# A fused top-k attention and Fourier-mix kernel: fewer key and value loads, and the attention output transposed by the DMA queue

## The chip, the cores and the metric

The kernel runs on one core of one Trainium2 chip. The metric is device time in microseconds for one execution of the whole program; less is better. The core has a matrix engine (TensorE, PE in the profile, with its weight loads shown apart as PEld), a vector engine (VectorE, DVE), an activation engine (ScalarE, ACT), a general engine (GpSimd, POOL) and SyncE (SP), which here does nothing but issue DMAs. Each engine works through its own list of instructions in order; where an instruction needs a result of another engine it waits, and everything behind it on the same engine waits too.

## The reference

Two blocks one after the other. Sizes: 8 batches, 8 heads, 576 tokens, head size 64; the model width is 512, and the hidden width of the MLP 2048. All is float32.

```python
def _attn_ref(q, k, v):
    scores = scale * np.matmul(q, k.transpose(0, 1, 3, 2))
    kth = np.partition(scores, -top_k, axis=-1)[..., -top_k:-top_k + 1]   # top_k = 32
    scores = np.where(scores >= kth, scores, -1000000000.0)
    scores = scores - np.max(scores, axis=-1, keepdims=True)
    attn = np.exp(scores)
    attn = attn / (np.sum(attn, axis=-1, keepdims=True) + 1e-09)
    return np.matmul(attn, v)

def _moe_ref(x, w_ch1, w_ch2):          # x: heads side by side, (8, 576, 512)
    X = np.fft.fft(np.fft.fft(x, axis=1), axis=2)
    u = x + np.real(X)
    un = (u - mean(u)) / np.sqrt(var(u) + 1e-06)
    return u + np.maximum(un @ w_ch1, 0.0) @ w_ch2
```

## The kernel before

The attention is worked in 32 pairs of heads (4 pairs to a batch). A pair has 9 items (`IN_PAIR`): the 576 queries are cut into four blocks of 128, of which each head is an item, and one block of 64 tail queries, in which both heads share an item. So there are 288 items, and the main loop (L1468) makes one step `i` for each: in step i VectorE finds the 32 largest scores of item i and begins those of item i+1 (four MAX8 and three MATCH_REPLACE8 per item, L406 and L408), while TensorE makes the scores of item i+3 (L382, L352), and ScalarE and GpSimd mask item i-1 (`mask`, L427 on ScalarE, L430 on GpSimd). `bounds` (L415) is one small GpSimd operation per item that turns the 32 maxima into the threshold `nt`; the mask of the next step needs it.

From pair 4 on, but for pairs 7 and 31 (`by_dma`), the probabilities are turned by DMA: ScalarE splits an item's float32 numbers into two planes of 16-bit words (`plane`, L451), SyncE writes them to DRAM (L464, or L466 to L468 for the tail item), and one step later issues a DMA transpose back into SBUF (`turn`, L484, tile `PT`). With them `attend` (L542) multiplies by the values. It runs for two chunks of a pair: chunk 0 (320 queries: two blocks and the tail) and chunk 1 (256 queries). Its result `o` lies in PSUM with the head dimension on the partitions, so it has to be turned once more and divided by the row sums. Before the change that is done so: in the step of `attend`, ScalarE copies `o` to `xT` (L556) and `rd` holds the reciprocals (L569); in a later step `to_tokens` has TensorE transpose `xT` into a PSUM tile `tpx` (L582, three transposes for chunk 0, two for chunk 1), and VectorE multiplies `tpx` by `rd` into `x` (L586, and L593 for the tail rows). For batch 1 the multiplication is on ScalarE (L605).

When a batch's attention is done, its `x` goes through the Fourier mix (GpSimd adds, `fold_ops`; TensorE products, L733, L790, L794), the normalisation, and the two layers of the MLP (L944; L971, L1010, L1141). The MLP is a list of units; each step takes so many units from the list as a planner (`level`, `fixed_cost`) finds room for beside the attention of later batches. The units of batch b are put on the list at its "arrival", a fixed number of steps after the step `T0` (L1360), so TensorE works on the MLP of one batch while the attention of the next ones runs. After the last item only the MLP of the last batch and what is left of the one before it remain.

SyncE's list in a step is: `turn` of item i-3, the planes of item i-2, pieces of the second weight matrix that units bring in (`bring`, L887), the loads of keys, queries or values for later pairs (`load_nat`, `load_v`: L237, L267, L277), and stores of results. GpSimd's list in a step is: the mask of item i-1, whatever is planned under "pool0" (folds), some sums for the MLP, `bounds(i)`, and more sums.

A chunk waits in the list `pending` until `to_tokens` may run: the step after its `attend`, no step with another `attend` in it, and for batches 2 and later only when the batch two before it has been stored, since `x` has two buffers.

Of the kernel before, what the change touches and what calls it, by code (L numbers as in the profile page):

```python
# [73 lines left out]
def kernel(  # L74
# [157 lines left out]

    def load_half(dst, src, pair, e, h, queue=None):

        b, hp = divmod(pair, NPB)
        s2 = src[b, 2 * hp + e].rearrange("(h r) d -> h r d", h=2)
        (queue or nc.sync).dma_start(  # L237
            out=dst[:, 2 * h:2 * h + 2, e, :],
            in_=s2[h, 0:2 * P, :].rearrange("(t p) d -> p t d", p=P),
        )  # L240

    def load_full(dst, src, pair):
        for e in range(2):
            for h in range(2):
                load_half(dst, src, pair, e, h)

    def load_tails(dst, src, pair, row0=(0, 0), queue=None, heads=(0, 1)):
        b, hp = divmod(pair, NPB)
        for e in heads:
            s2 = src[b, 2 * hp + e].rearrange("(h r) d -> h r d", h=2)  # L250
            for h in range(2):
                r0 = row0[e] + TH * h
                (queue or nc.sync).dma_start(
                    out=dst[r0:r0 + TH, NF, e, :], in_=s2[h, 2 * P:HS, :]
                )

    def heads_of(src, pair):
        b, hp = divmod(pair, NPB)
        return src[b, 2 * hp:2 * hp + 2].rearrange("e (h r) d -> h e r d", h=2)

    def load_nat(n, pair):
        if pair < NPAIR:
            nat[n, pair] = nat_t
            src = q if n == "q" else k
            load_full(nat_t, src, pair)
            for h in range(2):
                nc.sync.dma_start(  # L267
                    out=nat_t[TH * h:TH * (h + 1), NF, :, :],
                    in_=heads_of(src, pair)[h, :, 2 * P:HS, :].rearrange("e r d -> r e d"),
                )  # L270

    def load_v(pair):
        if pair < NPAIR:
            v_of[pair] = v_t[pair % 2]
            load_full(v_of[pair], v, pair)
            for e in range(2):
                nc.sync.dma_start(  # L277
                    out=v_of[pair][TAIL * e:TAIL * (e + 1), NF, e, :],
                    in_=heads_of(v, pair)[:, e, 2 * P:HS, :],
                )  # L280

# [40 lines left out]
    def scores(i, part):  # L322
# [14 lines left out]
        plain = (slice(0, NF * P), slice(NF * P, S))  # L337
        if e is None:
            to = [(Ssb[i], slice(TAIL * h, TAIL * (h + 1)), *plain) for h in range(2)]
        else:  # L340
            to = [
                (Ssb[i], slice(0, P), *plain),
                (Ssb[i + 1], slice(0, P), slice(TAIL, S), slice(0, TAIL)),
# [14 lines left out]
        if e is None and i >= PER_BATCH:  # L358
# [13 lines left out]
            for h, (s_t, r, _, _) in enumerate(to):  # L372
                for g in range(2):
                    nc.scalar.copy(  # L374
                        out=s_t[r, half * g:half * (g + 1)],
# [42 lines left out]

    def by_dma(i):

        pair = i // PER_PAIR
        return NPB <= pair < NPAIR - 1 and pair != 2 * NPB - 1
# [22 lines left out]
    def plane(i, half):  # L445
# [19 lines left out]
        else:  # L465
            nc.sync.dma_start(out=to[:, :, 0:S], in_=words[0:nq])  # L466
            nc.sync.dma_start(out=to[:, :, S:S + TAIL], in_=words[nq:P, :, NF * P:S])
            nc.sync.dma_start(out=to[:, :, S + TAIL:2 * S], in_=words[nq:P, :, 0:NF * P])  # L468
# [82 lines left out]
    def attended(pair, ch, late):  # L551
# [3 lines left out]
        xT = attp.tile([P, CW[0]], F32, name=f"xT_{pair}_{ch}", tag="xT", bufs=4)  # L555
        nc.scalar.copy(out=xT[:, 0:w], in_=o[:, 0:w])  # L556
        xT_of[pair, ch] = xT
# [14 lines left out]
    def to_tokens(pair, ch, at_once=True):  # L572
# [5 lines left out]
        xT, rd = xT_of.pop((pair, ch)), rd_of.pop((pair, ch))  # L578
        shape, name = [P, 4, P], f"tpx_{pair}_{ch}"
# [3 lines left out]
        cols = slice(P * hp, P * (hp + 1))  # L583
# [772 lines left out]
    for b in range(B):  # L1356
# [3 lines left out]
        T0 = end + (2 if first else 3 if soon else 4 if last else 5)  # L1360
# [107 lines left out]
    while i < N + 5 or plan or queue or sums:  # L1468
# [25 lines left out]

        if pending and pending[0][0] <= i and (
            i < 2 * PER_BATCH + 4 or chunk_at(i)[0] is None
        ):
            _, pp, pc = pending[0]
            if pp // NPB < 2 or pp // NPB - 2 in written:
                pending.pop(0)  # L1500
                tok.append(lambda: to_tokens(pp, pc, not short))
# [84 lines left out]
        for where in ("pool", "pool2", "load", "load2"):  # L1586
# [41 lines left out]
```

## Time and profile before

| | us |
|---|---|
| median of 3 runs | 1900.37 |
| lowest and highest of them | 1894.85, 1901.92 |
| the profiled execution | 1894.46 |
| its span, first to last instruction | 1892.7 |

The profile is of one execution. Its busy times per engine are sums over the span; an engine that is busy 90% of the time need not be the one that all wait for in every stage, so the stages are also shown one by one. In a list of waits, a line reads: engine and line that waited, the arrow, what it waited for, then us in total, number of waits, longest. In a table of windows each engine has its busy time and, in brackets, its instructions; PEclk is the clock that TensorE was granted, as a share of full speed. In a timeline a row is: start, us, engine, line, operation, out<-in, count, and in square brackets the idle time before it.

### The profile page before, as it was taken

To read this page: it belongs to the slowest core of one execution; us is meant where nothing else is said; L and a number is where in the kernel's file an instruction comes from. 1 tells how busy PE (TensorE), PEld (TensorE's weight loads), DVE (VectorE), ACT (ScalarE), POOL (GpSimd) and SP (SyncE) were. 2 spreads that over 40 slices of the span, in tenths; PEclk is the share of its full clock that TensorE was granted. 3 is DMA by queue.
4 is the path that set the end of the run, shared out by engine and by line. 5 is a ranking of instruction groups with operands and counts; after the bars stand their busy time and mean duration, and the time that the engine had idled before them with its cause. 6 is when DMAs were issued, how large, how long until landed. Compare 5 with 4: busy or idle time off the path is not lost.

```text
span 1892.7 us, 27288 instructions
## 1 busy us (share of the span) xinstructions
PE 1720.7 (91%) x8134; PEld 1086.8 (57%) x8134; DVE 1580.9 (84%) x3301; ACT 1296.3 (68%) x3104; POOL 911.6 (48%) x1278
## 2 busy tenths in 40 slices
PE   5667699889899999999999999999999999999999
PEld 3344364365456654566456665666556655667677
DVE  7999999699899999997998998998999999862110
ACT  6878658577787777776777687767787778652100
POOL 4768643354745356354643565355544465341012
PEclk8878899899899999999999999999999999999999
DMA  5333026561567755585465854585456755430132
GB/s 166 106 93 108 20 63 167 155 158 32 137 154 191 179 132 131 135 208 141 123 157 135 228 123 124 146 218 145 124 147 172 198 129 144 122 116 6 50 101 80
DMA packets 521972, 249.19 MB, mean 132 GB/s; under 512 B 403680, under 2 KB 511841, under 8 KB 521825
## 3 DMA queue, kind: packets, MB, share of 16 engines
q1 hardware_dynamic: 521040, 247.24, 50.1%
q8 instruction: 65, 1.06, 0.2%
q14 instruction: 83, 0.67, 0.1%
q10 hardware_dynamic: 784, 0.21, 0.0%
HBM read 93.63 MB, written 84.74 MB: 94 GB/s over the span
## 4 chain that ended last, share of the span: by engine, by line
PE 64%; DVE 11%; ACT 9%; DMA 6%; POOL 5%; issue 3%; SPq 2%; POOLq 0%; DVEq 0%; ACTq 0%
PE hp L944 23%; PE cp L971 9%; PE o L542 8%; DVE m L406 5%; PE sp L382 5%; DVE wk L408 5%; PE yp L733 3%; PE cw L1141 3%; PE cv L1141 3%; PE cp L1010 3%; ACT wk L451 2%; POOL wk L430 2%; ACT wk L427 2%; DMA PT<-planes 2%; PE sp_t L352 2%
## 5 line engine op out<-in xcount | busy, mean ns | idle before, releaser
L430 POOL TENSOR_TENSOR wk<-S,wk 128x576 f32<-128x576 f32 x288 | 408.1, 1417 | 570.0 <-ACT wk L427 564.7
L406 DVE MAX8 m<-wk 128x8 f32<-128x576 f32 x864 | 626.7, 750 | 6.0
L944 PE MATMUL hp<-unT,w 128*128 128x256 f32 (+1 forms) x2048 | 533.9, 411 | 3.3 <-ACT hT L948 2.5
L944 PEld LDWEIGHTS hp<-unT,w 128*128 128x128 f32 x2048 | 378.0, 191 | 133.7 <-issue 29.9
L408 DVE MATCH_REPLACE8 wk<-m,wk 128x576 f32<-128x576 f32 x576 | 427.5, 742 | 0.0
L451 ACT COPY wk<-S 128x576 uint16<-128x576 uint16 x468 | 288.7, 666 | 0.1
L427 ACT ACTIVATE wk<-S,nt 128x576 f32<-128x576 f32 x288 | 222.3, 772 | 72.1 <-POOL nt L415 71.1
L971 PE MATMUL cp<-w,hT 128*128 128x512 f32 x512 | 247.8, 621 | 0.0
L406 DVE MAX8 m<-S 128x8 f32<-128x576 f32 x288 | 214.0, 743 | 34.5 <-ACT S L356 34.3
L542 PE MATMUL o<-PT,v 128*64 128x256 f32 (+3 forms) x1440 | 206.4, 430 | 24.9 <-DMA PT<-planes 16.7
L408 DVE MATCH_REPLACE8 wk<-m,S 128x576 f32<-128x576 f32 x288 | 213.6, 742 | 0.0
L438 ACT ACTIVATE S<-wk,nt 128x576 f32<-128x576 f32 x234 | 182.6, 781 | 43.8 <-POOL wk L430 42.6
L948 ACT ACTIVATE hT<-hp 128x320 f32<-128x320 f32 (+1 forms) x256 | 103.6, 410 | 151.5 <-PE hp L944 150.8
L382 PE MATMUL sp<-kT,qT 64*128 64x512 f32 (+1 forms) x528 | 180.3, 680 | 13.1 <-ACT means L1329 5.1
L542 PEld LDWEIGHTS o<-PT,v 128*64 128x64 f32 x1440 | 118.5, 158 | 110.5 <-issue 30.1
L971 PEld LDWEIGHTS cp<-w,hT 128*128 128x128 f32 x512 | 94.1, 197 | 110.4 <-issue 108.6
L385 ACT COPY S<-sp 128x512 f32<-128x512 f32 (+1 forms) x264 | 141.8, 587 | 18.1 <-PE sp L382 17.2
L1086 POOL TENSOR_TENSOR hT<-hT 128x512 f32<-128x512 f32 x64 | 81.4, 1275 | 99.3 <-ACT hT L948 86.4
L415 POOL TENSOR_TENSOR nt<-m,cc 128x2 f32<-128x2 f32 x288 | 58.6, 204 | 117.9 <-DVE m L406 113.9
L352 PE MATMUL sp_t<-kt,qT 128*128 128x128 f32 x320 | 71.9, 308 | 44.8 <-ACT S L374 27.4
L352 PEld LDWEIGHTS sp_t<-kt,qT 128*128 128x128 f32 x320 | 55.6, 197 | 99.2 <-ACT S L374 41.7
L1141 PE MATMUL cw<-w,hT 128*128 128x256 f32 x448 | 105.8, 383 | 0.9 <-issue 0.6
(160 smaller groups left out, 2130.4 us busy)
## 6 DMA issues: line engine op xcount, KB each, us to landing
planes<-wk SPq DMA_DIRECT2D x208, 288.0 KB
w<-w_parts SPq DMA_DIRECT2D x82, 512.0 KB
space<-in_moe_w_ch_dram SPq DMA_DIRECT2D x32, 512.0 KB
nat<-in_q_dram SPq DMA_DIRECT2D x128, 64.0 KB
v<-in_v_dram SPq DMA_DIRECT2D x128, 64.0 KB
out_dram<-x SPq DMA_DIRECT2D x32, 256.0 KB
nat<-in_k_dram SPq DMA_DIRECT2D x124, 64.0 KB
w_parts<-w_t SPq DMA_DIRECT2D x8, 512.0 KB
```

Of the source, the lines that this page charges most:

```text
L352: nc.tensor.matmul(sp[:, 0:P], lhsT=qT[:, q_end - P:q_end], rhs=kt_t, start=True, stop=True)
L382: nc.tensor.matmul(sp[r], lhsT=qT[hd, q_cols], rhs=kT[hd, :], start=True, stop=True)
L406: ops.append(lambda src=src, m8=m8: nc.vector.max(out=m8, in_=src))
L408: ops.append(lambda src=src, m8=m8: nc.vector.match_replace(w, m8, src, NEG))
L427: nc.scalar.activation(out=w, in_=Ssb[i], func=AF.Relu, scale=-FAR, bias=Nt[i][:, 1:2])
L430: nc.gpsimd.tensor_tensor(out=w, in0=Ssb[i], in1=w, op=ALU.subtract)
L438: nc.scalar.activation(out=Ssb[i] if by_dma(i) else w, in_=w, func=AF.Exp, bias=Nt.pop(i)[:, 0:1], accum_out=den_t[pair % 3][:, c:c + 1],)
L451: nc.scalar.copy(out=words[:, half, :], in_=src[:, half, :])
L542: nc.tensor.matmul(o[D * e:D * (e + 1), c0:c1], lhsT=vv[:, c, e, :], rhs=pt[:, NF if c == NF else (NF + 1) * e + c, c0:c1], start=(c == 0) ...
L944: nc.tensor.matmul(hp[:, 0:w], lhsT=w1[:, dt, P * it:P * (it + 1)], rhs=unT[:, dt, 0:w], start=(dt == 0), stop=(dt == NDT - 1),)
L971: nc.tensor.matmul(cp, lhsT=hT[:, it, P * n:P * (n + 1)], rhs=w2[:, it, :], start=(it == 0), stop=(it == NIT - 1),)
L1141: nc.tensor.matmul(dst, lhsT=h()[a][:, kc, :], rhs=rhs_of(kc), start=start and kc == 0, stop=kc == NK - 1, skip_group_check=True,)
```

## The change

Three things change.

Keys and values are loaded in straight order. Before, a head's 576 rows were seen as two halves of 288, each with two blocks of 128 and 32 tail rows, for q, k and v alike. Now only q keeps that order; k and v are four blocks of 128 and a tail of 64. A pair's keys take 3 DMAs in place of 6, its values 4 in place of 6, and the planes of a tail item 2 in place of 3.

For the 26 pairs that `by_dma` covers, the output `o` is turned by DMA as well: ScalarE copies `o` in two copies, one for each half of the 32-bit words, SyncE writes both planes to a DRAM tile `oplanes` at the end of the step of `attend`, and in a later step `to_tokens` issues DMA transposes into `x`, under the new name "turn" at the very end of SyncE's list. Two steps on, GpSimd multiplies `x` by `rd` in place, under "pool0", which stands ahead of that step's `bounds`. TensorE's transposes and VectorE's (for batch 1 ScalarE's) multiplications of these pairs are gone. A step with another `attend` in it no longer holds such a chunk back.

Since `x` is complete later, T0 of batches 2 to 6 is two steps later; that of batches 0, 1 and 7 is as before.

```diff
     def load_half(dst, src, pair, e, h, queue=None):
-        b, hp = divmod(pair, NPB)
-        s2 = src[b, 2 * hp + e].rearrange("(h r) d -> h r d", h=2)
+        r0 = h * (HS if src is q else 2 * P)
         (queue or nc.sync).dma_start(
             out=dst[:, 2 * h:2 * h + 2, e, :],
-            in_=s2[h, 0:2 * P, :].rearrange("(t p) d -> p t d", p=P),
+            in_=head_of(src, pair, e)[r0:r0 + 2 * P].rearrange("(t p) d -> p t d", p=P),
         )
...
+            if n == "k":
+                for e in range(2):
+                    nc.sync.dma_start(
+                        out=nat_t[:, 0:NF, e, :],
+                        in_=both[e, 0:NF * P].rearrange("(c p) d -> p c d", p=P),
+                    )
+                nc.sync.dma_start(
+                    out=nat_t[0:TAIL, NF, :, :], in_=both[:, NF * P:S].rearrange("e r d -> r e d")
+                )
+                return
...
     def load_v(pair):
         if pair < NPAIR:
             v_of[pair] = v_t[pair % 2]
-            load_full(v_of[pair], v, pair)
             for e in range(2):
                 nc.sync.dma_start(
-                    out=v_of[pair][TAIL * e:TAIL * (e + 1), NF, e, :],
-                    in_=heads_of(v, pair)[:, e, 2 * P:HS, :],
+                    out=v_of[pair][:, 0:NF, e, :],
+                    in_=head_of(v, pair, e)[0:NF * P].rearrange("(c p) d -> p c d", p=P),
                 )
+            load_tails(v_of[pair], v, pair)
...
+    def pair_by_dma(pair):
+
+        return NPB <= pair < NPAIR - 1 and pair != 2 * NPB - 1
...
         else:
-            nc.sync.dma_start(out=to[:, :, 0:S], in_=words[0:nq])
-            nc.sync.dma_start(out=to[:, :, S:S + TAIL], in_=words[nq:P, :, NF * P:S])
-            nc.sync.dma_start(out=to[:, :, S + TAIL:2 * S], in_=words[nq:P, :, 0:NF * P])
+            for h in range(2):
+                nc.sync.dma_start(
+                    out=to[:, :, S * h:S * (h + 1)], in_=words[nq * h:nq * (h + 1)]
+                )
...
         o, w = o_of.pop((pair, ch)), CW[ch]
         PT.pop((pair, ch))
-        xT = attp.tile([P, CW[0]], F32, name=f"xT_{pair}_{ch}", tag="xT", bufs=4)
-        nc.scalar.copy(out=xT[:, 0:w], in_=o[:, 0:w])
-        xT_of[pair, ch] = xT
+        if pair_by_dma(pair):
+            words = attp.tile([P, 2, CW[0]], U16, name=f"ow_{pair}_{ch}", tag="xT", bufs=4)
+            src = o[:, 0:w].bitcast(U16).rearrange("p (s h) -> p h s", h=2)
+            for half in range(2):
+                nc.scalar.copy(out=words[:, half, 0:w], in_=src[:, half, :])
+            to = xT_of[pair, ch] = dramp.tile(
+                [P, 2, CW[0]], U16, name=f"oplanes_{pair}_{ch}", tag="oplanes", bufs=6
+            )
+            nc.sync.dma_start(out=to[:, :, TAIL:], in_=words[:, :, 0:2 * P])
+            if ch == 0:
+                nc.sync.dma_start(out=to[:, :, 0:TAIL], in_=words[:, :, 2 * P:])
+        else:
+            xT = attp.tile([P, CW[0]], F32, name=f"xT_{pair}_{ch}", tag="xT", bufs=4)
+            nc.scalar.copy(out=xT[:, 0:w], in_=o[:, 0:w])
+            xT_of[pair, ch] = xT
...
         xT, rd = xT_of.pop((pair, ch)), rd_of.pop((pair, ch))
+        cols = slice(P * hp, P * (hp + 1))
+        if pair_by_dma(pair):
+            rows = xT.rearrange("p h s -> (p h) s")
+            nc.sync.dma_start_transpose(
+                out=x[:, 2 * ch:2 * ch + 2, cols].bitcast(U16), in_=rows[:, TAIL:]
+            )
+            if ch == 0:
+                nc.sync.dma_start_transpose(out=x[:, 4:5, cols].bitcast(U16), in_=rows[:, 0:P])
+
+            def normalise_in_place():
+                for t0, nt, n, r in ((2 * ch, 2, 0, P), (4, 1, 4, TAIL))[:2 - ch]:
+                    xs = x[0:r, t0:t0 + nt, cols].rearrange("p t (e d) -> p t e d", e=2)
+                    by = rd[0:r, n:n + 2 * nt].rearrange("p (t e) -> p t e", e=2)
+                    nc.gpsimd.tensor_tensor(
+                        out=xs, in0=xs, in1=by.to_broadcast([r, nt, 2, D]), op=ALU.mult
+                    )
+
+            at(now[0] + 2, "pool0", normalise_in_place)
+            return 0.0
...
-        T0 = end + (2 if first else 3 if soon else 4 if last else 5)
+        T0 = end + (2 if first else 3 if soon else 4 if last else 7)
...
         if pending and pending[0][0] <= i and (
-            i < 2 * PER_BATCH + 4 or chunk_at(i)[0] is None
+            i < 2 * PER_BATCH + 4 or chunk_at(i)[0] is None or pair_by_dma(pending[0][1])
         ):
             _, pp, pc = pending[0]
             if pp // NPB < 2 or pp // NPB - 2 in written:
                 pending.pop(0)
-                tok.append(lambda: to_tokens(pp, pc, not short))
+                if not pair_by_dma(pp):
+                    tok.append(lambda: to_tokens(pp, pc, not short))
+                else:
+                    at(i, "turn", lambda: to_tokens(pp, pc))
...
-        for where in ("pool", "pool2", "load", "load2"):
+        for where in ("pool", "pool2", "load", "load2", "turn"):
             run(i, where)
```

## The prediction

> **What bounds the kernel now.** I read the head of the page, then busy time stage by stage, then the waits from the first pair turned by DMA to the end of the attention, then the chain of waits through the middle, and last the timelines of SyncE and GpSimd around one chunk. Head of the page, and chain by engine:
>
> ```profile
> span 1892.7 us, 27288 instructions
> PE 1720.7 (91%) x8134; PEld 1086.8 (57%) x8134; DVE 1580.9 (84%) x3301; ACT 1296.3 (68%) x3104; POOL 911.6 (48%) x1278
> PE 64%; DVE 11%; ACT 9%; DMA 6%; POOL 5%; issue 3%; SPq 2%; POOLq 0%; DVEq 0%; ACTq 0%
> ```
>
> TensorE carries two thirds of the chain. By stage (columns: window, length, busy of PE, PEld, DVE, ACT, POOL, clock, DMA share, GB/s):
>
> ```profile
> 480.00:770.00 290.00, 263.67 (x1273) 161.56 (x1274) 273.88 (x572) 224.11 (x533) 153.03 (x236) 0.95 0.62 155
> ...
> 770.00:1720.00 950.00, 916.49 (x4416) 584.88 (x4417) 841.46 (x1749) 696.86 (x1662) 462.12 (x680) 0.98 0.58 149
> ...
> 1700.00:1893.00 193.00, 188.15 (x851) 140.15 (x849) 28.07 (x69) 31.21 (x78) 30.68 (x50) 1.00 0.17 58
> ```
>
> From 480 to 770 us VectorE is the fuller engine (94%; TensorE 91%); these are the steps in which only the MLP of batch 1 is there to fill TensorE. From 770 us (the arrival of batch 2) to the end of the attention TensorE is busy 96% and VectorE 89%, and after 1700 us TensorE is alone. So in the first stage a saving on VectorE counts, later only one on TensorE: there the end is the sum of TensorE's work plus the 33.5 us that it idles. Waits between 450 and 1700 us:
>
> ```profile
> POOL wk L430 <- ACT wk L427: 472.3, 194, 15.0
> ACT xT L556 <- PE o L542: 84.7, 35, 12.1
> ...
> ACT wk L427 <- POOL nt L415: 62.4, 46, 3.8
> DVE x L586 <- PE tpx L582: 47.4, 17, 5.9
> ```
>
> The last line is what the change removes: VectorE's list stood still 17 times for TensorE's transposes. The line above it is where it may cost: ScalarE's mask waits for `nt`, and the new GpSimd work stands ahead of `nt`. Prices of TensorE's pieces come from the chain (start, us, what, how many):
>
> ```profile
> 907.41 2.84 PE o L542 x20
> ...
> 910.67 0.55 PE tpq L296 x5
> ...
> 985.50 2.31 PE o L542 x20
> ...
> 1000.61 0.33 PE tpx L582 x3
> 1000.93 1.06 PE sp L382 x4
> ...
> 1004.34 0.22 PE tpx L582 x2
> ```
>
> [...] a `tpx` transpose is listed with 273 ns (median), but three take 0.33 us of the chain, 0.11 each; I price by the chain. [...] All 130 transposes of the trace are SyncE's. [...] here a 128x256 one takes 728 ns on GpSimd (L1113) and 425 on VectorE (L586), 1.7 times.
>
> **TensorE's transposes.** 130 of the 160 go, 5 for each of 26 pairs, 0.55 us a pair. Between 770 and 1720 us there are 90, of which pair 31 keeps 5: 85 x 0.11 = 9.4 us, all on the path, since TensorE is the bound and takes other units in their place. The other 45 x 0.11 = 5 us lie where VectorE leads and count little.
>
> **VectorE's multiplications.** Between 480 and 770 us 11 of 0.42 us and 6 of 0.27 us go (6.2 us), with the waits just before them: 3.0 on TensorE, 1.6 on a store, 0.5 on `rd` (5 us). VectorE bounds that stage, but TensorE at 91% and ScalarE's chain follow close, so I take 7 of the 11 us. After 770 us VectorE loses 41.9 us of `tpx` waits and about 20 us of work, off the path; through earlier maxima, thresholds and masks it can remove some of TensorE's 33.5 idle us. Between 0 and 15; I take 5. In batch 1 ScalarE loses 30 multiplications of 316 ns (9.5 us) and gains six copies; it is at 70% there, so 1.5 us.
>
> **ScalarE's copies.** One copy of `o` (400 ns median) becomes two. No row shows a 16-bit read from PSUM. Planes from SBUF take 666 ns for 576 words, the masks 772 for 576 float32, so I take the same 400 ns for each: 52 x 0.4 = 21 us on an engine that has 253 idle us between 770 and 1720. The copy already waits for `attend` (84.7 us); the second delays the next step's masks by 0.4 us in 52 of 252 steps. Below nothing is excluded, since work is only added; the upper bound is 21. Inside the next item.
>
> **GpSimd's multiplications.** 52 of 0.73 us and 26 of 64x128 at 0.45 us (the row of 64x127 operands has 0.45): 50 us on an engine at 48%. They stand ahead of `nt`. In each of the 52 steps I measured from the trace how soon the mask starts after `nt`: in 19 it is within 0.8 us, so up to 19 x 0.95 = 18 us can reach ScalarE, and through it TensorE, whose products wait in three PSUM banks. In the others the idle time behind hides it. From 0 to 18 (39 with the copies); I take 4.
>
> **SyncE.** Per pair three loads of keys, two of values and one plane go, and three writes and three transposes come: the same count. A `PT` transpose of 256 rows and nine blocks takes 2.5 us to issue, so two blocks take about 0.6 and one 0.4 (estimates from that row); writes take 0.57. The load DMAs that remain carry twice the rows, so at most 2.5 us a pair are saved and 3.3 added. What SyncE does late has a deadline steps away: `PT` of the item turned behind an `oplanes` write is used four steps later, nor do keys or values fall due in the next step. Only `bring` is tight: TensorE waited 4.56 us for one at 1045. I add 1 us (0 to 6).
>
> **Is `x` there when GpSimd asks?** The timelines of one chunk, whose `attend` ends at 1015.5:
>
> ```profile
> 1022.55 0.88 SPq L267 DMA_DIRECT2D nat<-in_k_dram  x2
> ...
> 1026.41 2.81 SPq L484 DMA_TRANSPOSE PT<-planes  x1
> ```
>
> ```profile
> 1021.02 0.19 POOL L415 TENSOR_TENSOR nt<-m,cc 128x2 f32<-128x2 f32 x1 [2.26 <-DVE m L406]
> ...
> 1031.85 0.19 POOL L415 TENSOR_TENSOR nt<-m,cc 128x2 f32<-128x2 f32 x1 [0.26 <-DVE m L406]
> ```
>
> The step after `attend` ends on SyncE with the loads, at 1023.4. The new transposes stand there; the `nt` two steps on runs at 1031.85, 8.4 us later. Over all 52 chunks that distance is 6.1 us at the least and 9.7 in the median. The new chain needs 1.1 us for writes, 1.0 for transposes and some 2.5 to land (the larger `PT` transpose issued at 1026.41 keeps the queue busy until 1031, 1.8 us after its issue ends): 4.6 us, under 6.1. I charge no stall.
>
> **T0.** Batch 2 arrives two steps later, and until then VectorE sets the pace with TensorE's list of units already empty. A pair of such steps is not free: a step there takes 5.5 us (42 steps between the arrivals of batches 1 and 2, 537 to 769 us by their `nt`), and the attention's own work fills 1.4 us of it on TensorE. That is a ninth of a pair: four times 1.06 for scores and 0.22 for their tails, about 1.0 for the tail item, 2.84 and 2.31 for `attend`, twice 0.55 for turning queries and keys, 12.4 in all. What TensorE doesn't do in these two steps it does later, where it is the bound: 2 x (5.5 - 1.4) = 8 us. Batches 3 to 6 shift inside the TensorE-bound stage, where order doesn't change the sum. From 0, if TensorE has enough idle time left to catch up, to 8; I take 8.
>
> **Loads.** The bytes are the same, only the count of DMAs falls, and keys were never waited for after the start: 0.
>
> The sum: -9.4 - 7 - 5 - 1.5 + 4 + 1 + 8 = -10 us from the profiled execution's 1894.5, or 1884.5. The median of the runs is 1900.4, 0.3% above that execution; the same ratio gives 1890.
>
> **Rivals.** (1) The gain is larger. VectorE, relieved of 26 us of work and 47 of waits, shortens the loop VectorE, GpSimd, ScalarE, TensorE all along: TensorE's idle time falls by 15 in place of 5, the early stage gives all 11 in place of 7, GpSimd pushes nothing in place of 4, and T0 costs 4 in place of 8: 22 more, -32, 1868. For it: 15 of the 17 `tpx` waits lie in the late stage. Against it: TensorE is at 96% there already. (2) No change: the early stage gives 2, idle time nothing, and the push is 8: -9.4 - 2 - 1.5 + 8 + 1 + 8 = +4, 1904. For it: 46 waits of the mask for `nt`. (3) Slower: GpSimd stalls at the multiplication because the transposes land late; `nt` is behind it, and the mask, the exponential, the planes and the copies of the next scores are behind `nt` on ScalarE. For it: the smallest distance is 6.1 us, and the landing of the writes and transposes beside a 512 KB `bring` is an estimate. If landing takes some 5 us more, the median distance is used up; with 0.8 us of stall per chunk (42 us) and the full push of 18 in place of 4, -10 becomes +46: 1946. It decides from the point where pushes and stalls together cost over 24 us, 0.5 us a chunk (-10 - 4 + 24 = +10). Against it: `PT` is turned in nine blocks within about a step today, and TensorE waited for it 9 times in all.
>
> **Chances.** Forecast 0.50, rival 1 0.16, rival 2 0.10, rival 3 0.24. A measurement of this kernel tells a change from none at about 0.5%, 9.5 us, and the forecast lies on that line: 0.28 of its 0.50 is faster, 0.22 same. With rival 1 faster is 0.44; with rival 2 (0.08 same, 0.02 slower) and rival 3 (0.02 same, 0.22 slower) same is 0.32 and slower 0.24. The range runs from rival 1 at 1868 to 1916, where a push of 18 with none of the idle or the early gain puts the forecast (-9.4 - 1.5 + 18 + 1 + 8 = +16); most of rival 3 is left out. The forecast's own range is 1878 to 1902.
>
> **What would show it.** Right: no `tpx` for pairs 4 to 30 but 7; TensorE busy some 14 us less; VectorE's waits for `tpx` gone and its idle time now ahead of MAX8 on new scores; GpSimd some 50 us busier, with multiplications into `x` that wait for no DMA. Wrong: a line of GpSimd waiting for `oplanes`, ScalarE's waits for `nt` well over 62 us, TensorE's waits for `w` over 15 us, or TensorE less busy than 96% between 770 and 1700 us.

## The result, and the profile after

| | us |
|---|---|
| predicted | 1890 (1868 to 1916) |
| after, median of 4 runs | 1919.86 (1918.05 to 1930.06) |
| before, median of 4 runs beside them | 1897.61 (1889.99 to 1901.92) |
| ratio after to before | 1.0129, 95% interval 1.0098 to 1.0160 |
| the profiled execution after | 1920.23, its span 1918.4 |

The changed kernel is 1.3% slower, where a small gain was predicted. The head of the page after, and its chain of waits by engine:

```profile
span 1918.4 us, 26886 instructions
...
PE 1712.2 (89%) x8004; PEld 1078.6 (56%) x8004; DVE 1567.0 (82%) x3232; ACT 1303.8 (68%) x3126; POOL 948.6 (49%) x1356
...
PE 53%; ACT 11%; POOL 10%; DVE 8%; DMA 8%; issue 6%; SPq 4%; POOLq 0%; DVEq 0%; ACTq 0%
```

The 130 transposes are gone (8134 instructions to 8004) and TensorE is busy 8.5 us less, but the span is 25.7 us longer, so TensorE idles 34 us more (206.2 against 172.0). Its share of the chain fell from 64% to 53%; GpSimd, DMAs, SyncE's queue (SPq) and ScalarE took it over. Work was removed from the engine that sets the end, and that engine now stands and waits more. Its busy time fell by less than the transposes were worth, because its mean granted clock was 0.946 in this execution and 0.953 in that of before: counted at full clock (its busy time in quarters of a microsecond, each times the clock granted in it: 1644.1 us before, 1627.1 after), its work fell by about 17 us, and the lower clock took some 8 of them back. Busy time by stage (columns as before: window, length, busy of PE, PEld, DVE, ACT, POOL, clock, DMA share, GB/s):

```profile
480.00:770.00 290.00, 257.18 (x1210) 154.24 (x1208) 266.02 (x546) 221.82 (x534) 153.63 (x232) 0.93 0.65 161
770.00:1720.00 950.00, 896.52 (x4241) 565.52 (x4240) 837.77 (x1714) 703.74 (x1686) 490.94 (x739) 0.98 0.65 162
1700.00:1918.00 218.00, 212.30 (x971) 154.80 (x969) 41.02 (x95) 41.52 (x104) 40.60 (x64) 1.00 0.19 60
```

Before 770 us VectorE should have gained; it idles 24.0 of 290 us where it idled 16.1. After 770 us TensorE is busy 94.4% and was busy 96.5%: the prediction's own sign of being wrong. The waits of the changed kernel from 450 to 1700 us:

```profile
POOL wk L448 <- ACT wk L445: 520.8, 182, 11.4
DVE m L422 <- ACT S L372: 71.7, 46, 5.4
ACT wk L445 <- POOL nt L431: 63.1, 37, 4.8
ACT ow L578 <- PE o L561: 63.1, 30, 7.3
...
PE o L561 <- DMA PT<-planes: 19.1, 11, 4.8
```

Two lines of the kernel before that answer to the second and the last of these, from the same view:

```profile
DVE m L406 <- ACT S L356: 26.7, 14, 3.3
...
PE o L542 <- DMA PT<-planes: 7.7, 5, 3.0
```

VectorE's 47.4 us of waits for `tpx` are gone, and 45 us more of waits for the scores `S`, which ScalarE copies out of PSUM, have come in their place. TensorE waits 2.5 times as long for the probabilities `PT` that SyncE turns (over the whole run 26.3 us against 16.7). And SyncE now stands before its own new writes, for the operations behind ScalarE's copies (its queue's waits in the changed kernel, whole run):

```profile
SPq L582 <- ACT den L592: 88.2, 26, 7.1
...
SPq L582 <- ACT rd L599: 69.0, 26, 10.7
```

While it stands, what is behind it in its list is late too: in one case it stood 1.8 us for `rd` ahead of a write, which it issued at 1416.07, and two transposes into `x` (1416.66 and 1417.98) and one of `PT` (1419.33) came only behind that write. The sum of its standing did not grow, though: all waits of its queue between 450 and 1700 us add up to 504 us, and to 566 in the kernel before, there mostly (459) ahead of the writes and the turns of the planes of `PT`. What grew is the time its issues take: 60% of the stage from 770 to 1720 us, before 54%. One chunk in the timeline of the changed kernel:

```profile
1405.57 1.22 SPq L613 DMA_TRANSPOSE x<-oplanes  x1
...
1406.84 1.23 SPq L617 DMA_TRANSPOSE x<-oplanes  x1
...
1408.16 2.41 SPq L503 DMA_TRANSPOSE PT<-planes  x1
...
1412.84 2.38 PE L561 MATMUL o<-PT,v 128*64 128x256 f32 x20 [1.07 <-DMA PT<-planes]
...
1414.08 0.96 POOL L623 TENSOR_TENSOR x<-x,rd 128x256 f32<-128x256 f32 x2
```

The two new transposes take 2.45 us of SyncE's time directly ahead of the larger transpose of `PT`, and TensorE stands 1.07 us for that one. GpSimd's multiplication two steps on waits for nothing.

### The profile page after: what moved, and what is told of

Same layout as the page of the kernel before. It is cut to its first block, busy times and chain, and to the rows that moved or that the text cites. A ratio compares the mean times of both kernels' runs of the same rounds, so it can differ in the third digit from the quotient of the medians.

```text
span 1918.4 us, 26886 instructions
## 1 busy us (share of the span) xinstructions
PE 1712.2 (89%) x8004; PEld 1078.6 (56%) x8004; DVE 1567.0 (82%) x3232; ACT 1303.8 (68%) x3126; POOL 948.6 (49%) x1356
## 4 chain that ended last, share of the span: by engine, by line
PE 53%; ACT 11%; POOL 10%; DVE 8%; DMA 8%; issue 6%; SPq 4%; POOLq 0%; DVEq 0%; ACTq 0%
PE hp L993 21%; PE o L561 7%; PE cp L1020 5%; PE sp L398 4%; PE cw L1190 4%; DVE m L422 4%; POOL wk L448 4%; DVE wk L424 4%; PE cv L1190 3%; DMA PT<-planes 3%; ACT wk L445 2%; PE yp L782 2%; PE cp L1059 2%; DMA w<-w_parts 2%; ACT wk L469 2%
## 5 line engine op out<-in xcount | busy, mean ns | idle before, releaser
L1020 PE MATMUL cp<-w,hT 128*128 128x512 f32 x512 | 241.3, 610 | 0.0
L561 PE MATMUL o<-PT,v 128*64 128x256 f32 (+3 forms) x1440 | 205.9, 432 | 31.4 <-DMA PT<-planes 26.3
L398 PE MATMUL sp<-kT,qT 64*128 64x512 f32 (+1 forms) x528 | 176.0, 683 | 23.2 <-ACT S L372 8.4
L1190 PEld LDWEIGHTS cw<-w,hT 128*128 128x128 f32 x448 | 81.9, 190 | 27.1 <-issue 8.3
```

Of the source, the lines that this page charges most:

```text
L398: nc.tensor.matmul(sp[r], lhsT=qT[hd, q_cols], rhs=kT[hd, :], start=True, stop=True)
L561: nc.tensor.matmul(o[D * e:D * (e + 1), c0:c1], lhsT=vv[:, c, e, :], rhs=pt[:, NF if c == NF else (NF + 1) * e + c, c0:c1], start=(c == 0) ...
L1020: nc.tensor.matmul(cp, lhsT=hT[:, it, P * n:P * (n + 1)], rhs=w2[:, it, :], start=(it == 0), stop=(it == NIT - 1),)
L1190: nc.tensor.matmul(dst, lhsT=h()[a][:, kc, :], rhs=rhs_of(kc), start=start and kc == 0, stop=kc == NK - 1, skip_group_check=True,)
```

## The experiments

All ratios are to the kernel before, with a 95% interval; a hundredth is 19 us.

**1. The parts alone.** `loads_only` is the kernel before with the straight order of keys and values, T0 and the output path as before; `t0_only` is the kernel before with one expression changed:

```diff
-        T0 = end + (2 if first else 3 if soon else 4 if last else 5)
+        T0 = end + (2 if first else 3 if soon else 4 if last else 7)
```

> The kernel before with the keys and values in straight order alone; output path and T0 as before. If the loads are neutral, as the prediction has it: within 5 us of the kernel before. If fewer and larger loads hold up SyncE's queue or the transposes, part of the 24 us is here: 5 to 15 us slower. If they help: up to 5 us faster.

> The kernel before with T0 of batches 2 to 6 two steps later and nothing else. The prediction's term: 8 us slower. If the later T0 is the main loss: 15 to 25 us slower. If TensorE catches up: 0 to 3 us slower.

`loads_only`: 0.9956 (0.9933 to 0.9980), a gain of 8.4 us. `t0_only`: 1.0117 (1.0091 to 1.0143), a loss of 22 us. If the parts add, 1.0129 + 0.0044 - 0.0117 leaves 1.0056 for the output path, about 11 us; experiment 4 shows that they do not. In `loads_only` the DMAs that load queries, keys and values fall from 390 to 280 between steps 80 and 284, and their issues from 202 to 157 us of SyncE's time (added up from the two traces). The writes of planes fall from 244 to 222, and all of SyncE's issues in these steps from 661 to 596 us. The bytes are the same, so the gain goes with issues that are no longer there; that the issues make it, and not the other layout of the rows, was not tested.

**2. Two edits of the order.** `write_later` is the changed kernel with the writes of `oplanes` behind the planes of the next step; `norm_behind_nt` has GpSimd's multiplication behind `bounds`.

```diff
-            nc.sync.dma_start(out=to[:, :, TAIL:], in_=words[:, :, 0:2 * P])
...
+            at(now[0] + 1, "behind planes", write)
...
```

```diff
-            at(now[0] + 2, "pool0", normalise_in_place)
+            at(now[0] + 2, "pool", normalise_in_place)
```

> The changed kernel, but SyncE writes the planes of o behind the planes of the next step and not at the end of the step of attend, so that nothing stands behind a wait for attend. Theory SyncE (its queue stands still 157 us for ScalarE's copies of o, with turns and planes behind it): 12 to 24 us less than the changed kernel, 1896 to 1908. Rivals (GpSimd's work ahead of nt, the later T0, the transposes' own time): within 4 us of the changed kernel, 1916 to 1924.

> The changed kernel with GpSimd's multiplication behind the bounds of its step and not ahead of them. Theory GpSimd (each multiplication pushes nt and the mask): 10 to 18 us less than the changed kernel. Theory SyncE or T0: within 4 us of it.

`write_later`: 1.0105 (1.0081 to 1.0129), not to be told from the 1.0129 of the changed kernel. SyncE's standing of 157 us before the writes disappears from the list of waits, but its waits for planes ahead of `turn` rise from 89 to 173 us, and TensorE waits for `PT` as long as in the changed kernel (28.3 us in all, against 26.3). The standing was moved, not removed. `norm_behind_nt`: 1.0211 (1.0186 to 1.0235), a miss: taking the multiplication from ahead of `nt` did not gain, it cost 0.8% more. TensorE idles 67 us between 770 and 1720 us there, 53 in the changed kernel. TensorE's wait for `PT` is 38.7 us in it (26.3), and GpSimd's for `oplanes` 17.4 us (1.7). What behind `bounds` the multiplication delays was not settled.

**3. Which batches T0 costs.** `t0_batch2` moves batch 2 alone, `t0_batches3to6` the others, `t0_batches2to5` all but batch 6, each in the kernel before.

```diff
-        T0 = end + (2 if first else 3 if soon else 4 if last else 5)
+        T0 = end + (2 if first else 3 if soon else 4 if last else 7 if b == 2 else 5)
```

> The kernel before with T0 two steps later for batch 2 alone. Moving it for batches 2 to 6 together cost 1.17%, about 22 us: the attention ended 10 us later and the part behind the last item grew by 10 us. The prediction's theory: batch 2's arrival is the only one that costs, because VectorE sets the pace with no MLP units left before it; it gave 8 us, ratio 1.004, and if this part carries the whole cost 1.012. Rival: the cost lies with the later batches, whose units are pushed towards the end: then this run is within 0.2% of before, and the part behind the last item stays at 193 to 195 us.

> The kernel before with T0 two steps later for batches 3 to 6 alone. The prediction's theory says that these shift inside the stage in which TensorE is the bound and that order does not change the sum: within 0.2% of before. Rival: the planner has less room to spread the later units, so more are left when the last batch arrives, and TensorE idles just before each arrival: 1.007 to 1.012, with the part behind the last item at about 203 us as with all five batches moved, against 193.6 before.

> The kernel before with T0 two steps later for batches 2 to 5, batch 6 as before. Moved for 2 to 6 it was 1.0117, for 3 to 6 1.0081, for batch 2 alone 0.9962. Theory of the tail: the interval between the last two arrivals is two steps shorter when batch 6 is moved, the planner leaves 10 us more for the part behind the last item, and that is half of the cost: 1.004 to 1.007 here, with that part back at 193 to 194 us. Rival: the cost is TensorE's waits for w in each interval (4 us a batch), because the later units bring their weights in beside other transfers: 1.008 to 1.011, whatever the tail.

`t0_batch2`: 0.9962 (0.9944 to 0.9980). `t0_batches3to6`: 1.0081 (1.0064 to 1.0097). `t0_batches2to5`: 1.0110 (1.0079 to 1.0141). The prediction had it the other way round: the batch that was to cost gains 7 us, and those that were to be free cost 15. The effects do not add either: -0.4 and +0.8 make +1.2 together. The theory that the tail makes the loss falls with the third run: what follows the last item is back at 193.7 us (203.7 with batch 6 moved), but the attention itself then ends 22 us later in place of 10. The loss is only put elsewhere.

The page of `t0_batch2`, whose instructions are those of the kernel before:

```profile
span 1889.3 us, 27288 instructions
...
PE 1713.3 (91%) x8134; PEld 1084.2 (57%) x8134; DVE 1582.1 (84%) x3301; ACT 1295.6 (69%) x3104; POOL 913.8 (48%) x1278
```

The same 8134 matmuls take 7.4 us less than before (1720.7): the granted clock was 0.958 in this execution and 0.953 in that of before; over all runs 0.956 against 0.953. The span is 3.4 us shorter, so TensorE idles 4.0 us more. In these two executions, what batch 2 gains is the clock and not idle time. In `t0_batches3to6` it is the other way round: its profiled execution (span 1905.6, TensorE busy 1721.6) is 12.9 us longer, of which 12.0 are idle time; its clock was 0.947 over all runs. TensorE's share of the chain is 55% in the faster `t0_batch2` and 64% before, so that share alone doesn't tell a faster kernel from a slower one.

**4. The clock after a stall.** `t0_6` is the changed kernel with T0 one step later in place of two; so that its multiplications stay ahead of the folds of the same step, they stand under a name of their own. `last_by_pe` has T0 as before, with the last chunk of batches 2 to 6 (five of the 52) turned by TensorE and VectorE (in it, the sums over the tail rows read the last pair's rows before these are multiplied; the work is the same).

```diff
-            at(now[0] + 2, "pool0", normalise_in_place)
+            at(now[0] + 2, "norm", normalise_in_place)
...
-        T0 = end + (2 if first else 3 if soon else 4 if last else 7)
+        T0 = end + (2 if first else 3 if soon else 4 if last else 6)
...
+        run(i, "norm")
```

```diff
+    def out_by_dma(pair, ch):
+        return pair_by_dma(pair) and (pair % NPB, ch) != (NPB - 1, 1)
...
-        T0 = end + (2 if first else 3 if soon else 4 if last else 7)
+        T0 = end + (2 if first else 3 if soon else 4 if last else 5)
...
```

> The changed kernel with T0 one step later than before in place of two; the multiplications run directly ahead of the folds of the same step, so that the order of the two on GpSimd holds. Theory: T0 costs in proportion, 11 of its 22 us come back: 1.0129 - 0.0058 = 1.007 (1.005 to 1.009). Rival: the cost of T0 comes with the first step, or lies in the output by DMA: 1.011 to 1.015. Second rival: the cost comes with the second step alone: 1.001 to 1.003.

> The changed kernel with T0 as before; so that x is complete in time, the last chunk of each batch is turned by TensorE and VectorE as before, and the other 7 chunks of a batch by DMA. Theory: the three parts add up (loads -0.44%, T0 +1.17%, together 1.0129), which leaves +0.56% for the output by DMA; without T0 this gives 0.56 x 46/52 - 0.44, ratio 1.0005 (0.998 to 1.003). Rival: the output by DMA costs nothing on its own, and the rest of the loss comes from the late T0 meeting it: then the gain of the loads shows alone, 0.993 to 0.997. Second rival: it is the DMA path that costs, and T0 only where VectorE is still in it: 1.006 or more.

`t0_6`: 1.0180 (1.0162 to 1.0198). `last_by_pe`: 1.0156 (1.0141 to 1.0171). Both miss: with the output by DMA a nearer T0 is not cheaper but dearer, so these runs show no price per step of T0. Nor do the parts add: with T0 as before and the loads' gain of 0.44% in it, `last_by_pe` leaves about 2.0% for the output path, not 0.56%. So the 22 us of T0 hold in the kernel before; its share in the changed kernel isn't known. (One side effect stands in `t0_6`: the planner counts what is under "pool0", so it no longer counts the multiplications and may place more sums ahead of `bounds`.)

The head of the page of `t0_6`:

```profile
span 1928.5 us, 26871 instructions
...
PE 1721.0 (89%) x8004; PEld 1079.2 (56%) x8004; DVE 1565.5 (81%) x3232; ACT 1306.6 (68%) x3126; POOL 949.0 (49%) x1356
```

TensorE idles 207.5 us, hardly more than the 206.2 of the changed kernel, but its 8004 matmuls are busy 8.8 us longer (1712.2 there), at a mean clock of 0.940 against 0.946. So the loss of `t0_6` over the changed kernel lies in the clock. In `last_by_pe` TensorE idles 203.2 us and is busy 1718.3, at 0.940. The waits were exchanged: TensorE's for the weight pieces `w` are 28.3 and 24.4 us, against 11.2, those for `PT` 16.5 and 13.7, against 26.3, and the stalls for `w` are the longer ones, up to 7.2 us. One such stall in the timeline of TensorE in `t0_6`:

```profile
1062.65 1.07 PE L1059 MATMUL cp<-w,hT 128*64 128x512 f32 x2
1070.90 3.67 PE L1059 MATMUL cp<-w,hT 128*64 128x512 f32 x6 [7.17 <-DMA w<-w_parts]
...
1079.86 3.65 PE L1059 MATMUL cp<-w,hT 128*64 128x512 f32 x16
```

The eight products of L1059 that start from 1062.6 to 1073.5, six of them behind the stall, take 0.59 us at the least, 1.06 in the median and 1.11 at the most. (The rows of 6 and of 16 products in nearly the same time differ by more than that, and nothing is read from their counts.) The windows around it (clock is the last column but two):

```profile
1063.00:1071.00 8.00, 0.82 (x4) 0.11 (x4) 7.13 (x15) 0.00 (x0) 0.19 (x1) 0.72 0.93 262
1071.00:1075.00 4.00, 4.00 (x8) 1.15 (x10) 0.00 (x0) 0.00 (x0) 0.00 (x0) 0.50 0.60 154
1075.00:1080.00 5.00, 5.00 (x28) 1.85 (x27) 0.00 (x0) 2.28 (x6) 0.00 (x0) 0.83 0.00 0
1080.00:1085.00 5.00, 5.00 (x25) 1.79 (x25) 2.92 (x7) 3.78 (x12) 1.56 (x2) 1.00 0.57 129
```

The 0.72 and the 0.83 are means. The clock records of the traces of before and after hold two shares alone, 1.00 and 0.50. With these two, and one change in a window, the clock fell at about 1066.5 us (3.5 of the 8 us at 1.00 make 0.72) and was full again at about 1076.7 (1.7 of the 5 us at 0.50 make 0.83); both times are estimates from these windows. So it was halved about 2.8 us after TensorE's last product ended (1063.72), while TensorE stood, and was full only after about 5.8 us of work. In these 5.8 us the lower clock took an estimated 2.9 us of TensorE's work (5.8 x 0.50), beyond the 7.17 us of the stall, and no line of waits holds them. That the stall lowered the clock is suggested by this order, not shown.

**5. Is T0's cost the weight pieces?** `no_bring` is the kernel before without the weight transfers of batches 3 to 6 (TensorE multiplies by the pieces that batch 2 left; its work is the same), `t0_no_bring` the same with T0 moved for batches 2 to 6.

```diff
+        fetch = (lambda *of: None) if 3 <= b < B - 1 else bring
...
-                bring(T2, w2_12, part)
+                fetch(T2, w2_12, part)
...
```

> The kernel before without the transfers of second-layer weight pieces in the fast units of batches 3 to 6: TensorE multiplies by the pieces that batch 2 left, the output of these batches differs, the amount of work on every engine but SyncE is the same. It is the base for the next run. TensorE's waits for w are 7.2 us in the kernel before between 770 and 1720 us. Theory: they and the share of DMA traffic are small here, 0.994 to 0.999. Rival: w traffic is what holds this kernel in every interval: 0.990 or less.

> T0 two steps later for batches 2 to 6 (1.0117 against before) and the same transfers left out as in no_bring; to be read against no_bring. Theory: the cost of T0 in batches 3 to 6 is TensorE standing for w (18.7 us between 770 and 1720 us against 7.2)[...]; then the ratio of this run to no_bring falls from 1.0117 to 1.003 or less. Rival: the units meet the attention's own steps in a worse phase (waits for S, for PT, for the maxima), w is only where it shows: the ratio to no_bring stays at 1.008 to 1.013.

`no_bring`: 0.9910 (0.9891 to 0.9929), between the two expectations: 48 transfers fewer are worth 17 us, more than the 7.2 us of waits for `w` that the kernel before shows in that stage. They take both issues from SyncE and 25 of 249 MB of traffic away, and the run doesn't separate the two. `t0_no_bring`: 0.9985 (0.9974 to 0.9997). Its ratio to `no_bring` is 1896.32 / 1881.43 = 1.0079: of T0's 1.17% about a third goes with the weight pieces, two thirds stay (a rough share: each ratio is known to some 0.2%). TensorE's waits between 770 and 1720 us, in `t0_only`:

```profile
PE cp L1010 <- DMA w<-w_parts: 12.9, 4, 4.2
PE sp_t L352 <- ACT S L385: 10.0, 4, 3.3
PE sp_t L352 <- ACT S L374: 6.7, 11, 2.4
PE cw L1141 <- DMA w<-w_parts: 5.8, 3, 3.2
PE sp L382 <- ACT kT L306: 4.2, 2, 3.8
```

The same view of `no_bring`:

```profile
PE sp_t L352 <- ACT S L374: 13.4, 11, 2.3
PE cp L1010 <- DMA w<-w_parts: 6.6, 1, 6.6
...
PE sp_t L352 <- ACT S L385: 1.0, 1, 1.0
```

And of `t0_no_bring`:

```profile
PE sp_t L352 <- ACT S L385: 10.3, 5, 3.3
PE sp_t L352 <- ACT S L374: 6.8, 11, 2.4
PE sp L382 <- ACT kT L306: 4.3, 3, 3.5
```

Without the weight pieces the waits for `S` (L385) and `kT`, both copied out of PSUM by ScalarE, stay at 14.6 us; of these there is 1.0 us with the old T0. Those for the `S` of the tail items (L374) halve at the same time, from 13.4 to 6.8, so the three together explain 7 us; the rest is spread over small waits. TensorE idles 25.8 us in this stage in `no_bring` and 40.1 in `t0_no_bring`: 14.3 us, about the 14.9 by which the medians differ. So the order does change the sum, through TensorE's idle time.

**6. The output path piece by piece.** Each is the changed kernel (1.0129) with one piece edited. `no_norm` leaves out GpSimd's multiplication; `one_copy` makes one of ScalarE's two copies and writes it twice, so that the low words are lost:

```diff
-            at(now[0] + 2, "pool0", normalise_in_place)
+            at(now[0] + 2, "pool0", lambda: None)
```

```diff
-            for half in range(2):
-                nc.scalar.copy(out=words[:, half, 0:w], in_=src[:, half, :])
+            nc.scalar.copy(out=words[:, 1, 0:w], in_=src[:, 1, :])
...
+            high = words[:, 1:2, :].to_broadcast([P, 2, CW[0]])
...
```

> The changed kernel (1.0129) without GpSimd's multiplications: x is not divided by the row sums of the 26 pairs. The plan of the other GpSimd work is as in the changed kernel. Prediction's theory: standing ahead of nt they cost 4 us of at most 18, so 1.011. Theory now: the loop from VectorE's maxima over nt, ScalarE's mask and GpSimd's mask to the next scores has no slack in these steps (GpSimd's share of the chain of waits rose from 5% to 10%), so most of their 45 us beside nt comes back: 1.000 to 1.006. Rival: they are hidden, and the cost is ScalarE's copies or SyncE's order: 1.011 to 1.013.

> The changed kernel (1.0129) with one of ScalarE's two copies of o left out; SyncE writes the high words of o to both planes, so the output path moves the same bytes, but x does not hold the low words. Theory: the second copy delays the copies of the scores S on ScalarE, for which VectorE waited 72 us between 480 and 1720 us against 26 before; then this gives back 52 x 0.2 to 0.4 us, 1.002 to 1.008, and VectorE's waits for S fall below 50 us. Rival: the copies are hidden as predicted, and the waits for S only took the place of the waits for tpx: 1.010 to 1.013.

`no_norm`: 1.0110 (1.0091 to 1.0129), so the multiplication is hidden but for about 4 us, which can't be told from none. `one_copy`: 1.0077 (1.0052 to 1.0102): 10 us, but the intervals touch, so its size is uncertain. The sign by which this was to be known did not appear: VectorE's waits for `S` between 480 and 1720 us are 69.1 us, hardly less than 71.7. By the medians the second copy costs, but it does not make those waits.

`transposes_twice` issues each transpose of `oplanes` twice; `plain_copies` has plain DMA copies in their place, which leave out the turn and write the high words twice:

```diff
-            nc.sync.dma_start_transpose(
-                out=x[:, 2 * ch:2 * ch + 2, cols].bitcast(U16), in_=rows[:, TAIL:]
+            nc.sync.dma_start(
+                out=x[:, 2 * ch:2 * ch + 2, cols].bitcast(U16), in_=xT[:, 1:2, TAIL:].to_broadcast([P, 2, 2 * P]),
             )
...
```

> The changed kernel (1.0129) with each DMA transpose of the output issued twice: 3.7 us more of SyncE a pair, 97 us in all, and the traffic of the transposes doubled. Theory: SyncE's order is a part of the cost of the output path (TensorE waits 26 us for PT against 17 before, and the chain passes through SyncE's issues behind the masks); then doubling costs as much again as the path now loses beside the second copy, 5 to 15 us: 1.0155 to 1.021. Rival: SyncE has time enough and only ScalarE's second copy (0.52%) counts: 1.0115 to 1.0145.

> The changed kernel (1.0129) with plain DMA copies from oplanes into x in place of the 78 DMA transposes: the turn is left out, x holds high words in untransposed order, everything else stays. By the rows of a plain write (0.57 us to issue) against 1.28 and 1.23 us this takes 52 x 0.71 + 26 x 0.66 = 54 us from SyncE's issues and no instruction from any other engine. Theory: SyncE's list has no room left; doubling the transposes cost 5.7% for 97 us of issues and 77 us of standing between the pairs, 0.6 us per us, so some 10 to 30 us come back: 0.997 to 1.008. Rival: the cost of the doubling came from its own standing, and SyncE has room for the single set: 1.010 to 1.014.

`transposes_twice`: 1.0701 (1.0678 to 1.0724), far beyond both expectations. TensorE's wait for `PT` in the waits of that run:

```profile
PE o L561 <- DMA PT<-planes: 88.3, 27, 9.3
```

It is more than three times that of the changed kernel. But its SyncE queue has a new wait of its own, as each second transpose into the same `x` stands for the first:

```profile
SPq L614 <- DMA x<-oplanes: 76.7, 45, 5.4
```

So the run overstates one set. `plain_copies` has no such wait: 1.0037 (1.0020 to 1.0054). By the medians of their traces a copy takes 0.58 and 0.46 us to issue, where the transposes take 1.28 and 1.23: 52 x 0.70 + 26 x 0.77 = 56 us less for SyncE, and the kernel is 0.92%, 17 us, faster. From its waits:

```profile
DVE m L422 <- ACT S L372: 77.0, 45, 5.9
...
PE o L561 <- DMA PT<-planes: 19.2, 8, 5.9
```

TensorE's wait for `PT` is 19.2 us, against 26.3 in the changed kernel and 16.7 before. In the profiled executions TensorE idles 8.6 us less (197.6) and its matmuls are busy 4.5 us less (1707.7), at a clock of 0.952 against 0.946. That the DMA transposes cost more than plain DMAs is shown; whether by their issue time on SyncE, or also by what they do to other transfers in flight, these runs don't separate.

`write_on_act` issues the writes on ScalarE's queue:

```diff
-            nc.sync.dma_start(out=to[:, :, TAIL:], in_=words[:, :, 0:2 * P])
+            nc.scalar.dma_start(out=to[:, :, TAIL:], in_=words[:, :, 0:2 * P])
```

> The changed kernel (1.0129) with the writes of oplanes issued on ScalarE's queue, right behind ScalarE's copies: SyncE loses 78 writes (45 us of issues) and 157 us of standing for den and rd ahead of them. Theory of SyncE's list: TensorE's waits for PT fall from 26 to about 17 us, and the ratio to 1.002 to 1.009. Rival: ScalarE, which has the second copy already, pays for the issues: 1.012 to 1.025, with more waiting of VectorE for S than 72 us.

`write_on_act`: 1.0196 (1.0158 to 1.0234), the rival. From its waits:

```profile
DVE rd L600 <- ACT rd L599: 87.1, 29, 22.7
...
DVE m L422 <- ACT S L372: 81.6, 50, 7.4
```

TensorE's wait for `PT` is shorter (21.7 us), but VectorE waits 28 us more for `rd`, which ScalarE works out behind the two issues. By the medians, issues on ScalarE's queue were not free here either: 1.0196 against 1.0129 with them on SyncE.

**7. A version faster than both.** `loads_t0b2` is the kernel before with the loads in straight order and T0 later for batch 2 alone; the output stays with TensorE and VectorE.

> The kernel before with the loads in straight order (0.9956 alone) and T0 two steps later for batch 2 alone (0.9962 alone); the output by TensorE and VectorE as before. If the two gains add: 0.992 (0.990 to 0.994). Rival: both only shift the phase of the units against the attention, and together they give no more than one: 0.995 to 0.998, or nothing.

0.9922 (0.9901 to 0.9944), 1883.89 us against 1898.74: the two gains add. Its clock was 0.957 over all runs, against 0.951 of before. Of the 10.5 us by which its profiled execution is shorter (span 1882.2), 9.0 are TensorE's busy time, 1711.7 us for the same 8134 matmuls: most of the gain there is the clock too.

## Why the prediction was wrong

By its own steps:

- **TensorE's transposes, VectorE's multiplications and waits, batch 1** (-9.4, -7, -5, -1.5: 23 us together). TensorE's transposes, 9.4 us on the path and 5 before it, were priced about right: its work at full clock fell by about 17. (A transpose is listed with 273 ns, against 0.11 us of the chain; pricing by the chain held.) But the lower clock took half of that back, and the idle time was not used: TensorE idles 7 us more from 480 to 770 us and 20 more from 770 to 1720. VectorE's part was not measured by itself.
- **ScalarE's copies.** A copy takes 0.42 us (taken: 0.40). "Inside the next item", within 4 us, was too little by the medians: 10 us by `one_copy`, with the uncertainty named there.
- **GpSimd's multiplications.** 0.61 us each (taken: 0.73, from the 728 ns of GpSimd's 128x256 operation of L1113 in the kernel before). MAX8 on VectorE took 703 to 764 ns in the traces of before and of after alike. `no_norm` gives about 4 us, the figure predicted, but this can't be told from none.
- **SyncE, "I add 1 us (0 to 6)".** This is the step whose failure is shown in the changed kernel itself. The count of DMAs stayed the same, as predicted (848 and 849 between steps 80 and 284), but their issues grew from 661 to 734 us: the transposes' issue was estimated in proportion to their blocks, at 0.6 and 0.4 us, and it is 1.28 and 1.23. And it was argued that lateness is harmless since deadlines are steps away. `plain_copies` shows 17 us for the transposes over plain copies alone. SyncE's list was not full: its issues took 54% of the stage from 770 to 1720 us before, and 60% after. So a full list isn't the reason; that it is the order, what stands ahead of what, is argued and not shown. One line was misread here: at 1045 us TensorE did not wait 4.56 us for `bring`. That row of the chain is time of a DMA; TensorE's own timeline has products without a gap from 1045.05 to 1049.4. Its longest wait for a weight piece in the stage is 6.6 us, at 855.
- **Is `x` there when GpSimd asks?** Right: over the whole run GpSimd's multiplications wait once, 1.7 us, for the transposes out of `oplanes` (one mask is listed with 4.8 us behind a write of `oplanes`). Rival 3 had the sign but not the mechanism: GpSimd doesn't stall, and ScalarE's waits for `nt` are 63.1 us where they were 62.4.
- **T0, 8 us.** The other step that failed, and the larger error in the kernel before: 22 us by `t0_only`. "Batches 3 to 6 shift inside the TensorE-bound stage, where order doesn't change the sum" is what was wrong: they cost 15 us, nearly all of it idle time of TensorE (in the profiled executions 12.0 of 12.9 us; 41.9 us from 770 to 1720, before 33.5). Batch 2, taken as a loss of 8, is a gain of 7, in the profiled executions by the clock. How much of this is in the 24 us that the changed kernel loses stays open, as experiment 4 shows.
- **Loads, 0.** A gain of 8.4 us. The count of bytes was right; the gain goes with fewer issues, which were given no price.

What stays open: how the late T0 and the output by DMA act on each other; which step's meeting of units and attention makes T0's two thirds that aren't weight pieces; and what makes VectorE's waits for `S`, since neither the second copy nor the multiplication nor the writes on SyncE, taken away one at a time, brought them down.

## What to carry to other kernels

A queue that only issues DMAs was far from full here, its issues took 60% of the stage from 770 to 1720 us, and still 78 transposes in place of plain copies cost 17 us. Before you call an addition to such a queue free, ask what stands behind it in the list and is needed soon, and price an issue by a row of its own size, not in proportion from a larger one (here 0.6 us in proportion, 1.28 measured). With one engine busy 96% it still mattered where its work stands: a hand-planned order, shifted by two steps in four batches, cost 15 us, and with five batches shifted TensorE waited 18.7 us for weight pieces between 770 and 1720 us, before 7.2. Such shifts are to be tried one at a time, as some gain and some lose. When busy time differs for the same instructions (here 1713.3 and 1720.7 us for 8134 matmuls, at mean clocks of 0.958 and 0.953), look at the clock before you look for a cause in the waits. Undo a bundle of edits part by part, and in both orders, since the parts need not add: here one part of a change that loses 1.3% gains 0.4%, and another gains as much in one batch and loses twice that in the others.

## What the hardware showed unexpectedly

- A DMA transpose of 256 rows and two blocks of columns took 1.28 us to issue on SyncE, with one block 1.23; plain copies into the same places 0.58 and 0.46. From issue to landing the medians were 3.0 us for the larger transpose and 2.7 for its copy. So the two were near each other from issue to landing, and not in the issue.
- After one stall of 7.17 us TensorE worked about 5.8 us at a granted clock of 0.50 (worked out from the windows of experiment 4). Two kernels with the same 8134 matmuls differed by 7.4 us in TensorE's busy time (1720.7 and 1713.3), with mean clocks of 0.953 and 0.958.
